# Chunked delta rule feeding a maxout FFN on one core: an earlier load and scaling of the second chunk's values, and small products moved to other places among the FFN's matmuls

## The chip, the cores and the metric

One core of one Trainium2 chip. The metric is the device time in microseconds (us) of one execution of the whole program. In the text PE is the matmul engine (TensorE), DVE the VectorE, ACT the ScalarE, POOL the GpSimd, SP the SyncE; each runs its own instructions strictly in the order in which the kernel's Python code emits them.

## The reference

A gated delta rule runs over 768 tokens for 4 x 8 heads of width 48. Its outputs are laid out as 3072 tokens of width 384 and go through a maxout FFN.

```python
k_n = k / (np.linalg.norm(k, axis=-1, keepdims=True) + 1e-06)
state = np.zeros((B, H, D, D))                  # B, H, S, D = 4, 8, 768, 48
for t in range(S):
    kt, vt, bt = k_n[:, :, t], v[:, :, t], beta[:, :, t, None]
    y[:, :, t] = np.einsum('bhd,bhde->bhe', q[:, :, t], state)
    v_old = np.einsum('bhde,bhd->bhe', state, kt)
    state = state + bt[:, :, :, None] * np.einsum('bhd,bhe->bhde', kt, vt - v_old)
x = y.transpose(0, 2, 1, 3).reshape(3072, 384)
h = np.maximum(np.maximum(x @ w1, x @ w2), x @ w3)   # w1, w2, w3: 384 x 768
out = h @ w_out                                      # w_out: 768 x 384
```

All is float32; the four FFN weights arrive as float64 and are turned into float32 on the chip.

## The kernel before, in words

**Chunks and groups.** The sequence is cut into 12 chunks `c` of 64 tokens. A chunk has two units `n = 2c + g` (g picks the batches). Two chunks make a group `m`; there are 6 groups (`GROUPS`). Within a chunk the recurrence is solved in closed form: products of keys with keys and with queries (`gram`, p_g, tiles `at` and `pt`), a triangular inverse, and a few products with the running state `st`.

**The inverse** (`solve(m)`, a generator) works on 32 x 32 blocks for a whole group: norms and beta are put together (`inverse_square`, L278 to L283, and L582), `norm` on POOL (L286 to L292) makes the key norms, one multiply over the block tile (L599, 128 x 1024) scales it, and 31 steps `j` follow of a product (L617) and a subtraction (L621) each on DVE. Each `yield` is a place where the emitting code can stop; `some(solving, n)` emits n pieces. At step `j == 1` DVE turns the norms (`norms_of`, L318). For group 0, `first_norms` has the norms of chunks 0 and 1 in `nrm_0`.

**The recurrence of chunk c** is a row of short links, each with its letter in the order tables: `e` and `f` (only in the first group) are `halves_z` (p_e, L740) and `halves_u` (p_f, L751, its negation on ACT at L755); `z` is `join_z` (p_z, L768, copies on ACT at L772); `d` is `turn_t1` (three transposes on DVE, L685 and L687); `j` is `join_u` (p_j, L781, which needs z's copies and d's transposes; ACT negates it at L783); `k` is `old_k` (p_k, L798, the state times the keys, subtracted on DVE from the scaled values `v_t` at L810); `q` is `old_q` (p_q, L798, copied by ACT at L818); `u` is `new` (p_u, L826, which needs j's result and k's); `y` is `to_y` (p_y, L868, added to q's copy on DVE at L870); `s` is `step` (p_s, L849, added into `st` on DVE at L856); `x` is `to_x` (p_x). `T` and `P` in the first table are the transposes and the score products (`gram`) of the queries of one unit, `M` a mask on DVE, `S1` one piece of `solving`.

**The values** `v_t` of a chunk come by two DMAs (`load_v`, L148) and are multiplied by the norms (`scale`, L324; on POOL for c up to 9).

**The FFN of group m** (`ffn(m)`, a generator) has products p_h (L1311), one *unit* per `yield`, followed by a copy on ACT (L1319, L1321) or a maximum on DVE (L1325), and then output products p_o (L1354; in the last three groups L1040). In group 0 a unit is 256 tokens wide. The weights are converted piece by piece meanwhile (`weights`): three ACT operations (L255 to L257) on a fetched piece, a shift on DVE (L266), an addition on POOL (L270); `fetch` (L224) issues the DMA of a piece, `join_last` emits the shift and the addition of the last piece begun. Unit number k of the first units needs piece k.

**The order.** The schedule is written out by hand. The main loops walk over the yields of `ffn(m)`, and at iteration `i` emit what the tables name: `FIRST` and `EARLY_LINKS` (with `SOLVED` for the substitution) beside `ffn(0)`, `LINKS`, `FOURTH_LINKS` and `LAST_LINKS` beside the later ones, where `X` is `turn_y` (L927, a DVE transpose that makes the next group's `xt` from outputs that went through DRAM: `y_blocks` L906 and `read_y` L916, letters x and w), `K` is `load_k` (there on the POOL queue) and `P` is `prep_values`. So moving a name to another iteration moves its place in the program order of every engine and queue that it uses.

Of the kernel before, what the change touches and what calls it, by code (L numbers as in the profile page):

```python
# [23 lines left out]
def kernel(  # L24
# [31 lines left out]
    nc = tc.nc  # L56
# [35 lines left out]
    def ps_two(name):  # L92
        return pairs.tile([128, 2, 512], FP32, name=name, tag="two", bufs=3)
# [24 lines left out]
    def rows(bb):  # L118
        return slice(C * bb, C * (bb + 1))
# [16 lines left out]
    def place(n):  # L136
        return n % NK if n < 12 else n % 4
# [4 lines left out]
    def load_q(n, queues=one_queue):  # L142
        load(q, qpad[n % NQ], n, queues)

    def load_v(c, queue=nc.sync):
        vts[c] = work.tile([128, 2, H, D], FP32, name="v_t", bufs=3)
        for bb in range(2):
            queue.dma_start(  # L148
                out=vts[c][rows(bb)].rearrange("p g h d -> p (g h) d"),
                in_=v[2 * bb : 2 * bb + 2, :, c * C : (c + 1) * C, :].rearrange(  # L150
                    "b h p d -> p (b h) d"
                ),
            )
# [78 lines left out]
    def join_last():  # L232
        if waiting:
            joined(*waiting.pop())
# [29 lines left out]
    def joined(dst, mant, mant_v, up_v):  # L264

        nc.vector.tensor_scalar(  # L266
            out=mant, in0=mant, scalar1=3, scalar2=None,
            op0=ALU.logical_shift_left,
        )
        nc.gpsimd.tensor_tensor(  # L270
            out=dst.bitcast(I32), in0=mant_v.bitcast(I32), in1=up_v, op=ALU.add
        )
# [50 lines left out]
    def scale(c, nrm):  # L323
        (nc.vector if c > 9 else nc.gpsimd).tensor_tensor(  # L324
            out=vts[c], in0=vts[c],
            in1=nrm[:, :, :, None].to_broadcast([128, 2, H, D]), op=ALU.mult,
        )
# [7 lines left out]
    nrm_0 = const.tile([128, 2, 2, H], FP32, name="nrm_0")  # L335
# [8 lines left out]
    def square(name):  # L344
        return work.tile([128, H, C], FP32, name=name, tag="square", bufs=17)
# [4 lines left out]
    def turn(n, parts=(0, 1), copy=nc.scalar.copy):  # L350

        if n not in kqts:
            if n == 6:
                kqts[n] = work.tile([128, KT, TOK], FP32, name="xt").rearrange(
                    "p k t -> p (k t)"
                )[:, 0 : NP * 4 * C].rearrange(
                    "p (j b i t) -> p j b i t", b=2, i=2, t=C
                )
            else:
                kqts[n] = work.tile([128, NP, 2, 2, C], FP32, name="kqt", bufs=6)  # L360
        kqt = kqts[n]
        p_t = ps_two("p_t")
        for i in parts:
            src = (kpad[place(n)], qpad[n % NQ])[i]
            for j in range(NP):
                nc.tensor.transpose(  # L366
                    p_t[:, i, j * 128 : (j + 1) * 128],
                    src[:, 2 * j : 2 * j + 2],
                    ident,
                )  # L370
        some = slice(parts[0], parts[-1] + 1)
        copy(  # L372
            kqt.rearrange("p j b i t -> p i (j b) t")[:, some],
            p_t.rearrange("p i (x t) -> p i x t", t=C)[:, some],
        )
# [56 lines left out]
    def gram(n, parts=(0, 1), queues=one_queue, copy=nc.scalar.copy, later=False):  # L432
        kqt, g = kqts[n], n % 2
        p_g = ps_two("p_g")

        whole = len(parts) == 2 and not g
        for j in range(NP):
            for par in range(2):
                for bb in range(2):
                    kq = kqt[dims(par), j, bb ^ g]  # L440
                    for i in (0,) if whole else parts:
                        c0 = j * 128 + i * C
                        nc.tensor.matmul(  # L443
                            p_g[
                                rows(bb ^ (g * i)), par, c0 : c0 + C * (1 + whole)
                            ],
                            kq[:, 0],
                            kq if whole else kq[:, i],
                        )
        p_v = p_g.rearrange("p two (j i t) -> p two j i t", j=NP, i=2)  # L450
        if 1 in parts:
            pt = pts[n] = square("pt")
            if later:
                return lambda: copy(by_par(pt), p_v[:, :, :, 1])
            else:
                masked(pt, p_v[:, :, :, 1])
        if 0 not in parts:
            return
        at = ats[n] = square("at")
        copy(by_par(at), p_v[:, :, :, 0])  # L460
        if queues:
            to_dram(n, queues)
# [96 lines left out]
    def solve(m):  # L559
# [34 lines left out]
        else:  # L594
            size, xv, yv = BL, x[:, None], y[:, None]
            xb, by = x, bl[:, None, :].to_broadcast([128, BL, BL])
        if m == 2:
            yield
        nc.vector.tensor_tensor(out=xb, in0=xb, in1=by, op=ALU.mult)  # L599
        yield  # L600
        for j in range(size - 1):
# [5 lines left out]
            n = BL // size  # L607
# [86 lines left out]
    def halves_t(c, parts=(0, 1)):  # L694
        if c not in fine:
            fine[c] = [square("t") for g in range(2)]
        src = [ut[c % NU][:, g].rearrange("p h x -> p (h x)") for g in range(2)]
        dst = [t.rearrange("p h x -> p (h x)") for t in fine[c]]
        if 0 in parts:
            nc.vector.transpose(out=dst[0], in_=src[0])  # L700
        for bb in range(2) if 1 in parts else ():
            nc.vector.transpose(out=dst[1][rows(1 - bb)], in_=src[1][rows(bb)])
# [684 lines left out]
    def keys(n, queues=one_queue, copy=nc.scalar.copy):  # L1387
        gram(n, (0,), queues, copy)
# [40 lines left out]
    turn(7, (0,))  # L1429
    turn(1, (1,))  # L1430
    keys(7)
    turn(2, (1,))
    gram(1, (1,), None, later=True)()
    some(conv, 1)
# [20 lines left out]
    for n in range(2):  # L1455
# [3 lines left out]
    new(0)  # L1459
    some(conv, 1)  # L1460
    fetch(nc.gpsimd)
    load_v(1, nc.gpsimd)
    placed(1, 3)
    to_y(0)
    busy(2, ident)
    join_last()
    halves_t(1)
    solving = solve(1)
    some(solving, 1)
# [7 lines left out]
    LINKS = {  # L1477
        0: "k0 q0 t0 L3", 1: "t1", 2: "g0 g1 t2", 3: "t3", 4: "z0 z1 d0 d1 V0",
        5: "g2 g3 p1", 6: "j0 j1 N0", 7: "u0 V1 N1", 8: "N2", 9: "s0 y0", 10: "x0",
        11: "k1 q1", 12: "u1 w0", 14: "y1 x1 s1", 15: "X0 w1", 16: "P0",  # L1480
        18: "X1 K0 K1 K2 K3",
    }
    FOURTH_LINKS = {
        **LINKS, 15: "w1", 16: "X0", 18: "", 19: "X1",
        21: "P0 K0 K1 K2 K3",
    }
    LAST_LINKS = {
# [11 lines left out]
    EARLY_LINKS = {  # L1499
        9: "k0 q0", 10: "t0", 11: "t1", 12: "g0", 13: "t2", 14: "g1", 15: "t3",  # L1500
        16: "g2", 17: "g3", 20: "d0 d1 z0 z1", 22: "j0", 24: "j1 u0", 26: "s0",
        28: "k1 q1", 29: "y0 u1", 30: "s1 x0", 31: "y1",
    }


    FIRST = {
        0: "S1 S1", 1: "e1 s0 S1 S1 S1", 2: "f1 k1 M2 S1 S1",
        3: "z1 d1 S1 M3 S1 S1", 4: "j1 q1", 5: "u1 T4", 6: "y1 s1 T5", 7: "x1 T6",
        8: "T7", 14: "P4", 15: "P5", 26: "P6", 27: "P7", 30: "P9 P11",
    }  # L1510


# [26 lines left out]
    def queries(names):  # L1539
# [12 lines left out]
    FETCHED = {8: 1, 12: 1, 13: 1, 14: 1, 21: 2, 22: 1, 23: 1, 24: 1, 25: 1}  # L1552
    LESS = {3: 0, 6: 1, 9: 2, 18: 3, 21: 4, 25: 5}
    SOLVED = {
        **{i + 4: n for i, n in enumerate((3, 2, 2, 2, 3, 3, 3, 3, 2, 2))},
        27: 1, 28: 1, 29: 1, 30: 6, 31: 17, 32: 6, 33: 5,
    }
    for i, _ in enumerate(ffn(0)):
        if i < 7:
            fetch(nc.sync if i else nc.gpsimd)  # L1560
        if i == 0:
            scale(1, nrm_0[:, 1])
        if i == 1:
            load_q(4)
            load_q(5)
        if i == 2:
            load_q(6)
        if i < 6 or i == 16:
            join_last()
        for _ in range(FETCHED.get(i, 0)):  # L1570
            fetch(nc.gpsimd)
        queries(FIRST.get(i, ""))
        links(1, EARLY_LINKS.get(i, ""))
        if i == 26:
            solving = solve(2)
            some(solving, 1)
        if i in CONVERTED:
            some(conv, 1 + (i == 22))
        if i == 0:
            fetch(nc.gpsimd)  # L1580
        some(solving, SOLVED.get(i, 0))
        if i in (8, 13):
            prep_values(i // 4)
        if i in (4, 8):
            for n in range(2):
                load_k(8 + 2 * (i > 4) + n, (nc.gpsimd, nc.gpsimd))
        if i == 11:
            load_q(11, (nc.gpsimd, nc.gpsimd))
        if i in (3, 9, 10, 21):
            load_v((3, 9, 10, 21).index(i) + 2)  # L1590
        if i == 18:
            blocks(2)
        if i == 30:
            prep_values(4)
        if i in (29, 30, 31):
            load_blocks(i - 17, nc.sync)
        if i in LESS:
            less_first(LESS[i], nc.gpsimd if i < 10 else nc.vector)
        if i in (30, 31):
            turn_first((2 * i - 60, 2 * i - 59))  # L1600
        if i == 31:
            turn_first((4, 5))
            for t in range(KT):
                both_layers(t)
                if t == 0:
                    links(1, "x1")
# [55 lines left out]
```

## Time and profile before

| what | before |
|---|---|
| time, median of 3 runs (lowest to highest) | 501.86 us (499.53 to 503.12) |
| the profiled execution's own time | 502.37 us |
| its span from first to last instruction | 500.7 us |
| PE busy, share of the span | 478.0 us, 95% |
| DVE, ACT, POOL busy | 348.6, 169.3, 197.9 us |
| mean granted TensorE clock | 0.981 |

The profiled execution took 1.67 us more than its span. A share of busy time is a mean over very different stretches: up to about 43 us the group 0 inverse runs and PE waits for DVE and ACT; between 43 and 70 us the first FFN units run between the links of chunk 1; from 70 us on PE is nearly always busy. A row of the timeline gives the start, the duration, the engine, the line and the tiles of one or more like instructions, and in square brackets the idle time before it with what released it.

### The profile page before, as it was taken

Reading aid. Unit: us, or ns where it says so; the run is one execution under the profiler, and the core shown is the slowest. Engines: PE = TensorE matmul, PEld = TensorE weight load, DVE = VectorE, ACT = ScalarE, POOL = GpSimd, SP = SyncE. Lnnn points to the kernel's source line nnn. Section 1 sums busy time; section 2 is a strip of 40 time slices with the busy share of each in tenths; the row PEclk is TensorE's granted clock in tenths of the full one; section 3 lists DMA queues with packets and bytes.
Section 4 is the critical chain, followed back from the end, with each engine's and each line's share of the span. In section 5 each row is a group of like instructions: output and inputs, shape, how many; then the busy total and the mean of one; then the engine's idle time right before and its main releaser. Section 6 shows DMA issues by size and latency. Waiting matters only on the chain.

```text
span 500.7 us, 18774 instructions
## 1 busy us (share of the span) xinstructions
PE 478.0 (95%) x8100; PEld 341.6 (68%) x8100; DVE 348.6 (70%) x819; ACT 169.3 (34%) x329; POOL 197.9 (40%) x334
## 2 busy tenths in 40 slices
PE   7669889999999999999999999999999999999995
PEld 6558678887765555665555564655797457998895
DVE  4888978765687361979551998565998865467843
ACT  5776755985230135111234110243211042113210
POOL 6557693864660393871574880601000020000000
PEclk9958899999999999999999999999999999999999
DMA  8948979874351654454765453833224321330001
GB/s 112 162 102 223 207 185 129 199 203 90 90 137 36 138 116 108 120 125 121 154 133 114 116 158 90 164 56 83 65 57 96 61 66 28 87 81 1 1 16 48
DMA packets 109603, 53.52 MB, mean 107 GB/s; under 512 B 92752, under 2 KB 103344, under 8 KB 109520
## 3 DMA queue, kind: packets, MB, share of 16 engines
q1 hardware_dynamic: 97824, 31.62, 31.4%
q0 software_dynamic: 9280, 20.11, 16.0%
q8 instruction: 64, 1.05, 0.9%
q10 hardware_dynamic: 2416, 0.59, 0.7%
q14 instruction: 19, 0.16, 0.1%
HBM read 39.17 MB, written 13.11 MB: 104 GB/s over the span
## 4 chain that ended last, share of the span: by engine, by line
PE 87%; DVE 8%; issue 2%; ACT 1%; DMA 1%; SPq 0%; POOL 0%; DVEq 0%; POOLq 0%; ACTq 0%
PE p_h L1311 34%; PE p_o L1040 12%; PE p_o L1354 11%; PE p_c L1249 5%; PE p_g L443 4%; PE p_u L826 3%; PE p_y L868 3%; PE p_k L798 2%; PE p_m L960 2%; PE p_q L798 2%; PE p_t L366 2%; PE p_s L849 2%; PE p_z L768 2%; PE p_j L781 2%; DVE tmp L617 2%
## 5 line engine op out<-in xcount | busy, mean ns | idle before, releaser
L1311 PE MATMUL p_h<-xt,w_sb 128*128 128x512 f32 (+1 forms) x468 | 176.8, 523 | 1.3 <-DVE tmp L617 0.9
L1311 PEld LDWEIGHTS p_h<-xt,w_sb 128*128 128x128 f32 x468 | 85.4, 191 | 64.2 <-issue 54.8
L1325 DVE TENSOR_TENSOR h<-h,p_h 128x512 f32<-128x512 f32 (+1 forms) x42 | 23.9, 569 | 44.8 <-PE p_h L1311 43.1
L621 DVE TENSOR_TENSOR y_bl<-y_bl,tmp 128x31 f32<-128x31 f32 (+20 forms) x139 | 48.6, 350 | 4.8
L617 DVE TENSOR_TENSOR tmp<-x_bl,y_bl 128x31 f32<-128x31 f32 (+20 forms) x139 | 47.0, 338 | 4.1
L1354 PE MATMUL p_o<-wo_sb,h 128*128 128x384 f32 x144 | 49.8, 491 | 0.0
L1321 ACT ACTIVATE h<-p_h 128x512 f32<-128x512 f32 (+1 forms) x30 | 16.6, 552 | 84.8 <-PE p_h L1311 80.2
L401 POOL DMA_DIRECT2D turned<-in_q_dram x72 | 39.2, 552 | 4.2 <-POOL turned L396 3.4
L1354 PEld LDWEIGHTS p_o<-wo_sb,h 128*128 128x128 f32 x144 | 26.7, 190 | 17.3
L443 PEld LDWEIGHTS p_g<-kqt 48*64 48x64 f32 x1184 | 22.7, 134 | 11.4 <-issue 7.7
L443 PE MATMUL p_g<-kqt 48*64 48x64 f32 (+1 forms) x1184 | 25.9, 234 | 2.6 <-ACT kqt L372 2.6
L270 POOL TENSOR_TENSOR w_sb<-mant,up 128x384 int32<-128x384 int32 x18 | 18.5, 1030 | 23.9 <-DVE mant L266 19.9
L396 POOL MEMSET turned<- 128x96 f32 x18 | 3.3, 189 | 56.6 <-DVE kqt L417 56.6
L653 POOL DMA_DIRECT2D ut<-y_d x4 | 2.6, 650 | 57.8 <-DMA y_d<-y_bl 57.8
L148 POOL DMA_DIRECT2D v_t<-in_v_dram x14 | 11.6, 830 | 34.5 <-PE p_u L826 34.5
L1360 ACT COPY o_sb<-p_o 128x384 f32<-128x384 f32 x12 | 5.7, 478 | 56.0 <-PE p_o L1354 50.6
L1354 PE MATMUL p_o<-w_sb,xt 128*128 128x384 f32 x60 | 21.0, 486 | 0.0
L810 DVE TENSOR_TENSOR v_t<-v_t,p_k 128x768 f32<-128x768 f32 x11 | 10.5, 950 | 15.0 <-PE p_k L798 15.0
L427 DVE TENSOR_TENSOR pt<-p_g,mask 128x512 f32<-128x512 f32 x20 | 13.6, 688 | 10.2 <-PE p_g L443 9.9
L401 POOL DMA_DIRECT2D turned<-in_k_dram x32 | 17.5, 553 | 3.3 <-DMA v_t<-in_v_dram 1.9
L460 ACT COPY at<-p_g 128x512 f32<-128x512 f32 x22 | 12.7, 583 | 17.7 <-DVE pt L427 16.2
L826 PEld LDWEIGHTS p_u<-v_t,ut 64*64 64x64 f32 x768 | 13.5, 142 | 6.7 <-issue 6.1
(254 smaller groups left out, 920.8 us busy)
## 6 DMA issues: line engine op xcount, KB each, us to landing
w_bits<-in_moe_w_dram SPq DMA_DIRECT2D x9, 384.0 KB, 5.8
w_bits<-in_moe_w_dram POOLq DMA_DIRECT2D x9, 384.0 KB, 5.4
turned<-in_q_dram POOLq DMA_DIRECT2D x72, 48.0 KB, 2.5
out_dram<-o_sb SPq DMA_DIRECT2D x34, 96.0 KB, 2.3
y_x<-y SPq DMA_DIRECT2D x30, 96.0 KB, 2.6
qall<-y_x SPq DMA_DIRECT2D x30, 96.0 KB, 2.8
v_t<-in_v_dram POOLq DMA_DIRECT2D x14, 192.0 KB, 4.6
at_d<-at SPq DMA_DIRECT2D x76, 32.0 KB, 3.0
```

The costliest lines, as they stand in the source:

```text
L270: nc.gpsimd.tensor_tensor(out=dst.bitcast(I32), in0=mant_v.bitcast(I32), in1=up_v, op=ALU.add)
L401: (queue, nc.gpsimd)[i].dma_start(out=t[p0 : p0 + 32, bb, at : at + NP * 2 * D].rearrange("p (j x) -> p j x", j=NP), in_=(k, q)[i][2 * bb ...
L443: nc.tensor.matmul(p_g[rows(bb ^ (g * i)), par, c0 : c0 + C * (1 + whole)], kq[:, 0], kq if whole else kq[:, i],)
L617: nc.vector.tensor_tensor(out=t_v, in0=row.to_broadcast(t_v.shape), in1=column.to_broadcast(t_v.shape), op=ALU.mult,)
L621: nc.vector.tensor_tensor(out=rest, in0=rest, in1=t_v, op=ALU.subtract)
L798: nc.tensor.matmul(p_b[rows(bb), par, c0 : c0 + D], kqt[g][dims(par), j, bb ^ g, i], st[dims(par), bb ^ g, g, j],)
L826: nc.tensor.matmul(p_v[rows(bb ^ g), g, i], ut[c % NU][rows(bb), g, h], rhs[rows(bb), g, h],)
L1040: nc.tensor.matmul(to[:, g], a[j][:, 128 * g : 128 * (g + 1)], b[j], start=(start and g == of[0] and j == 0), stop=(stop and g == of[-1] a ...
L1249: nc.tensor.matmul(to, w[stays], moves, start=(n == 0), stop=(n == len(terms) - 1))
L1311: nc.tensor.matmul(p_h, w_sb[i][:, t, f * 128 : (f + 1) * 128], xt[:, t, lo : lo + w], start=(t == 0), stop=(t == KT - 1),)
L1325: nc.vector.tensor_tensor(out=h, in0=h, in1=p_h, op=ALU.max)
L1354: nc.tensor.matmul(p_o, stays, moves, start=(n == 0), stop=(n == len(terms) - 1))
```

## The change

`load_v(1)` is emitted earlier and on the SP queue, behind `keys(7)`, where before it came behind `new(0)` on the POOL queue. `scale(1)` is emitted ahead of `halves_t(1)` and `solve(1)`, so on POOL it stands ahead of `norm`; before it stood in iteration 0 of the loop over `ffn(0)`. `solve(1)` gets one more place to stop, ahead of the multiply at L599, as `solve(2)` has. The tables get other places: the substitution of group 1 begins in iteration 1 instead of in `solve(1)`'s first piece and iteration 0, and is level with the old order again behind iteration 5; `k1` goes from iteration 2 to 3 (beside `z1`), `q1` from 4 to 6 (beside `y1`); `y0` of chunk 2 from 29 to 27, `P6` and `P7` from 26 and 27 to 23 and 25. In `LINKS`, `X1` and the four `K` go from iteration 18 to 17; in `FOURTH_LINKS`, `X1` goes from 19 to 18.

```diff
@@ solve(m)
-        if m == 2:
+        if m in (1, 2):
             yield
         nc.vector.tensor_tensor(out=xb, in0=xb, in1=by, op=ALU.mult)
         yield
@@ ahead of the loops
     keys(7)
+    load_v(1)
     turn(2, (1,))
     gram(1, (1,), None, later=True)()
     some(conv, 1)
...
     new(0)
     some(conv, 1)
     fetch(nc.gpsimd)
-    load_v(1, nc.gpsimd)
     placed(1, 3)
     to_y(0)
     busy(2, ident)
     join_last()
+    scale(1, nrm_0[:, 1])
     halves_t(1)
     solving = solve(1)
     some(solving, 1)
@@ LINKS, FOURTH_LINKS
-        18: "X1 K0 K1 K2 K3",
+        17: "X1 K0 K1 K2 K3",
     }
     FOURTH_LINKS = {
-        **LINKS, 15: "w1", 16: "X0", 18: "", 19: "X1",
+        **LINKS, 15: "w1", 16: "X0", 17: "", 18: "X1",
@@ EARLY_LINKS
-        28: "k1 q1", 29: "y0 u1", 30: "s1 x0", 31: "y1",
+        27: "y0", 28: "k1 q1", 29: "u1", 30: "s1 x0", 31: "y1",
@@ FIRST
-        0: "S1 S1", 1: "e1 s0 S1 S1 S1", 2: "f1 k1 M2 S1 S1",
-        3: "z1 d1 S1 M3 S1 S1", 4: "j1 q1", 5: "u1 T4", 6: "y1 s1 T5", 7: "x1 T6",
-        8: "T7", 14: "P4", 15: "P5", 26: "P6", 27: "P7", 30: "P9 P11",
+        1: "e1 S1 s0 S1 S1", 2: "f1 S1 S1 S1 M2", 3: "k1 z1 d1 S1 M3 S1 S1",
+        4: "j1", 5: "u1 T4", 6: "q1 y1 s1 T5", 7: "x1 T6",
+        8: "T7", 14: "P4", 15: "P5", 23: "P6", 25: "P7", 30: "P9 P11",
@@ SOLVED
-        **{i + 4: n for i, n in enumerate((3, 2, 2, 2, 3, 3, 3, 3, 2, 2))},
+        **{i + 4: n for i, n in enumerate((4, 3, 2, 2, 3, 3, 3, 3, 2, 2))},
@@ loop over ffn(0)
         if i < 7:
             fetch(nc.sync if i else nc.gpsimd)
-        if i == 0:
-            scale(1, nrm_0[:, 1])
```

## The prediction

> **What bounds the kernel now.** I read the page first, then the windows table by stage, then the timeline of each engine between 40 and 70 us, then PE's timeline to the end for rows with idle time.
>
> The windows table (us, then busy time and instructions of PE, PE's weight loads, DVE, ACT, POOL, then the granted clock, DMA share, GB/s):
>
> ```profile
> 50.00:55.00 5.00, 3.33 (x133) 2.72 (x132) 4.64 (x11) 2.98 (x8) 4.27 (x5) 0.97 1.11 228
> 55.00:60.00 5.00, 5.00 (x116) 3.59 (x114) 4.77 (x13) 3.79 (x8) 2.65 (x4) 0.68 1.19 209
> 60.00:65.00 5.00, 3.70 (x131) 3.01 (x128) 4.72 (x14) 4.24 (x8) 3.58 (x5) 1.00 0.77 190
> 65.00:70.00 5.00, 4.30 (x152) 3.75 (x155) 2.96 (x7) 2.96 (x6) 4.73 (x6) 1.00 0.51 114
> 75.00:80.00 5.00, 5.00 (x144) 4.31 (x143) 4.72 (x13) 1.77 (x3) 1.42 (x2) 1.00 1.35 155
> ```
>
> From 70 us to the end PE has no idle time worth naming except at 120 us (0.55 and 0.30) and at 310 us. So an order change can win only what PE loses between 43 and 70 us: 1.67 us idle in 50 to 55, 1.30 in 60 to 65, 0.70 in 65 to 70, and a clock of 0.68 in 55 to 60. DVE is busy over 4.6 of 5 us there: it has next to no slack.
>
> PE's timeline there and at 310 us:
>
> ```profile
> 48.48 0.31 PE L849 MATMUL p_s<-u,kpad 64*64 64x48 f32 x2 [0.26 <-issue]
> 51.99 1.02 PE L798 MATMUL p_k<-st,kqt 48*64 48x48 f32 x55 [0.64 <-DVE st L856]
> 54.05 0.37 PE L798 MATMUL p_k<-st,kqt 48*64 48x48 f32 x9 [1.03 <-issue]
> 54.34 2.57 PE L1311 MATMUL p_h<-xt,w_sb 128*128 128x256 f32 x6
> 60.72 0.39 PE L781 MATMUL p_j<-z,t 32*32 32x32 f32 x23 [0.68 <-issue]
> 65.70 0.68 PE L826 MATMUL p_u<-v_t,ut 64*64 64x48 f32 x30 [1.31 <-issue]
> 66.80 1.46 PE L1311 MATMUL p_h<-xt,w_sb 128*128 128x256 f32 x6
> 310.46 2.81 PE L1311 MATMUL p_h<-xt,w_sb 128*128 128x512 f32 x6 [0.87 <-DVE tmp L617]
> ```
>
> Only 0.64 us of it is a wait for another engine. Three pauses are "issue". Between them lie 126 and 127 matmuls (9 + 6 + 64 + 6 + 41, then 23 + 64 + 6 + 34), and 127 between the pause at 48.48 and the one at 54.05: a pause every 254 instructions, counting weight loads. The unit at 54.34 took 2.57 us where the one at 66.80 took 1.46.
>
> Why DVE's addition into st came late (POOL, DVE and ACT timelines):
>
> ```profile
> 42.37 1.68 POOL L148 DMA_DIRECT2D v_t<-in_v_dram  x2
> 49.39 1.47 POOL L324 TENSOR_TENSOR v_t<-v_t,nrm 128x768 f32<-128x768 f32 x1 [0.72 <-DVE y_p L621]
> 50.82 1.10 POOL L270 TENSOR_TENSOR w_sb<-mant,up 128x384 int32<-128x384 int32 x1
> 49.57 1.50 DVE L266 TENSOR_SCALAR mant<-mant 128x384 uint32<-128x384 uint32 x1
> 50.99 0.94 DVE L856 TENSOR_TENSOR st<-st,p_s 128x768 f32<-128x768 f32 x1
> 51.96 0.57 ACT L255 ACTIVATE mant<-w_bits 128x384 f32<-128x384 f32 x1 [4.04 <-POOL w_sb L270]
> ```
>
> The values were asked for at 42.37 to 44.05; L148's DMAs land in 3.7 to 6.0 us, so `scale` on POOL began at 49.39. DVE's shift, 0.35 us elsewhere, took 1.50 beside it, and L856 stood behind the shift. POOL's addition waited behind `scale`, ACT's conversion for that, and behind ACT's conversion stood the negation of p_f (53.42).
>
> **The load.** Two issues leave POOL (1.68 us) and two join SP behind the eight writes of `at` that end at 30.63; L148 on SP took 2.21 us for two. SP's next instruction, a fetch, then waited 11.4 us for its buffer, which hides the 2.2; without that cover piece 8 would come 2.2 us later. The values land by about 39 us (32.8 + 6.0). They could push the block read that POOL asks for at 36.13: ACT waited 0.6 us for it and had 0.65 us spare before its next wait. DMA share from 30 to 35 us is 0.09, so I take 0; bounds 0 and 2 us (384 KB at the 190 GB/s of the busy windows).
>
> **The scaling.** POOL's addition of piece 2, at 44.05 before, starts at 42.4, `scale` runs 43.4 to 44.9, the norm follows; its third operation waits for DVE's reciprocal (45.8) as before. L289 took 1.24 us beside the multiply L599; with the multiply put off I take 0.3, as its neighbours. POOL is free at 47.2 instead of 47.9, issues a fetch (0.8) and adds piece 3 at 48 to 49.5 instead of 50.8 to 51.9. ACT's conversion moves from 51.96 to about 49.6 and the negation from 53.42 to 51.3, right behind p_f.
>
> **k beside z.** p_s ends at 48.8; DVE now has the shift of piece 4 and the multiply done by 48.5, so st is ready at 49.8. PE reaches p_k only after the next unit, at 52.6. The 0.64 goes. With it the half clock should go: single-us windows show 0.50 from 55 to 58, after a stretch from 51.4 to 54.8 in which PE worked 1.8 of 3.4 us. That half clock cost 2.57 - 1.46 = 1.1 at 54.34 and about 0.3 in the next two groups: **1.4 us**; bounds 0 (the stretch moves on) and 1.4.
>
> **What is late next.** DVE. From 46.2 until d1's transposes are done it must run three shifts (0.35 each), two maxima (0.4), the multiply (1.15), st (0.9), steps 0 to 4 (0.4, 0.45, 0.55, 0.6, 0.65), the norm turn (0.85), a mask (0.68), one more shift, k's subtraction (0.95), d1 (1.36): 10.8 us, and about 0.8 of waits (for p_s, for ACT's conversion of piece 6): 57.8. PE without pauses would be at p_j at 56.2, with one pause of 0.5 at 56.7. So p_j waits **1.1 us**; behind it stand unit 5 and p_u. Bounds 0 (if DVE is spared its waits) and 1.6. u then needs j's negation (ACT, 1.2 us), hidden by unit 5 (1.4).
>
> **The issue pauses** (1.03 + 0.68 + 1.31 = 3.02). The number of instructions is unchanged, so pauses remain. With a DMA share of 0.2 at 120 us they were 0.55 and 0.30. 384 KB leave the window from 42 to 49 us, which moves the whole backlog up. I take 2.2 in all, **0.8 less**; bounds 0.9 (three of the quiet ones) and 5 (below). [...]
>
> **q beside y, P6, P7, y0.** No work is added. q's copy on ACT (0.80) ends under p_y (1.1) before L870 needs it; without that cover y is 0.8 later. P6, P7 and y0 lie where PE is busy 10.0 of 10 us: 0, with 0.5 either way for the two pauses at 120.
>
> **X1 and K.** At 310.46 PE waits for L927, which began at 309.11 behind three substitution steps that iteration 17 emits (3 x 0.68 us). Put ahead of them it could begin at 307.1; its data were asked for at 302.11 to 304.67, and land 2.8 us later (the median of that queue's row), by 307.5. It ends at 308.7 and the **0.87** goes; bounds 0 and 0.87. The three steps end 0 to 0.4 us later, with no one waiting. The K issues (8 on POOL, 0.69 each, by L129's row) start one iteration earlier on an engine busy under half the time: 0. In `FOURTH_LINKS` no DVE instruction stands between iterations 18 and 19: 0.
>
> **The sum**, against the profiled time: 502.37 - 0.64 - 1.4 + 1.1 - 0.8 - 0.87 = 499.8. The median of the runs lies 0.5 below the profiled one; I give **499.4**.
>
> **Rivals.** [...]
>
> [...]
>
> (3) *More comes back.* p_j does not wait, and pauses fall to the quiet 0.9: 502.37 - 0.64 - 1.4 - 0.87 - 2.1 = 497.4, 496.9 on the runs' level, less if the pauses at 120 us go too. For: DVE's waits may vanish, the DMA backlog shortens; against: DVE 4.7 of 5 us.
>
> **Chances.** Forecast 0.37, rival (1) 0.14, (2) 0.21, (3) 0.28. 1% is 5.0 us, about what a measurement of this kernel can tell from no change. Faster by more (under 496.8): 0.22 of (3) and 0.04 of the forecast, 0.26. Slower by more (over 506.9): 0.10 of (2) and 0.04 for what I do not see, 0.14. The rest, 0.60, is within 1%. The range reaches from (3) to (2): 495.8 to 505.0.
>
> **What would show it.** Right: `scale` of chunk 1 on POOL near 43.4 at 1.5 us; L856 before 50; no DVE wait ahead of p_k; a clock of 1.00 from 54 to 58; p_j waiting about 1 us for L687; the unit after the third p_o group without idle near 308. Wrong: a clock of 0.5 in another window between 56 and 70; pauses that sum to 3 us or more; PE starting its first unit later than 43.3; DVE stopping for DMA at L927.

## The result, and the profile after

The change makes the kernel slower: 504.10 us (median of 22 runs, 499.86 to 508.27) against 501.23 us (22 runs of the kernel before on the same chip, 498.23 to 504.58), a ratio of 1.0054 with a 95% interval of 1.0033 to 1.0076. The ratios here and below leave out the few executions in a slower state (three of the 22 of the change, 507.53 to 508.27 us), so they need not be the quotient of two medians. The profiled execution of the changed kernel took 504.63 us, its span 502.5; before it was 502.37 and 500.7. What follows explains these two executions, 1.8 us apart in their spans where the medians lie 2.9 us apart.

The windows table of the changed kernel (us, then busy time and instructions of PE, weight loads, DVE, ACT, POOL, then granted clock, DMA share, GB/s):

```profile
50.00:55.00 5.00, 3.57 (x119) 2.91 (x119) 4.69 (x18) 3.61 (x9) 1.80 (x2) 1.00 1.16 233
55.00:60.00 5.00, 4.48 (x126) 3.36 (x126) 4.39 (x11) 2.71 (x5) 2.91 (x3) 0.66 1.02 183
60.00:65.00 5.00, 3.77 (x116) 3.12 (x106) 4.69 (x14) 3.08 (x6) 3.28 (x5) 1.00 0.76 212
65.00:70.00 5.00, 3.80 (x156) 3.14 (x155) 4.00 (x9) 3.35 (x7) 4.64 (x6) 1.00 0.75 171
70.00:75.00 5.00, 3.75 (x50) 3.37 (x50) 2.19 (x5) 0.59 (x1) 3.24 (x5) 0.52 0.39 114
75.00:80.00 5.00, 5.00 (x26) 4.36 (x26) 3.20 (x9) 1.71 (x3) 2.20 (x3) 0.79 0.61 113
```

Between 70 and 80 us, where PE ran at full clock without a pause before, the clock is now 0.52 and 0.79, and PE is idle 1.25 us. Between 70 and 75 us DVE falls to 2.19 busy of 5 and ACT to 0.59: both wait for PE (DVE 3.4 us for p_s, ACT 5.4 us for p_t). PE's timeline names the places:

```profile
55.52 0.45 PE L798 MATMUL p_k<-st,kqt 48*64 48x48 f32 x16 [1.94 <-issue]
56.58 2.93 PE L1311 MATMUL p_h<-xt,w_sb 128*128 128x256 f32 x6
61.39 0.39 PE L781 MATMUL p_j<-z,t 32*32 32x32 f32 x24 [1.23 <-issue]
66.16 1.15 PE L798 MATMUL p_q<-st,kqt 48*64 48x48 f32 x64
67.13 1.11 PE L868 MATMUL p_y<-u,pt 64*64 64x48 f32 x64
68.41 0.56 PE L849 MATMUL p_s<-u,kpad 64*64 64x48 f32 x22 [0.16 <-ACT qs L818]
71.25 1.41 PE L849 MATMUL p_s<-u,kpad 64*64 64x48 f32 x42 [2.29 <-issue]
73.50 2.76 PE L1311 MATMUL p_h<-xt,w_sb 128*128 128x256 f32 x6
290.33 1.26 PE L826 MATMUL p_u<-v_t,ut 64*64 64x48 f32 x64 [1.12 <-POOL kmore L396]
```

No wait for DVE is left between 44 and 68 us, as intended, but the pauses called "issue" have grown from 3.28 us (the prediction's three, 3.02, and 0.26 in p_s at 48.48) to 5.46. The new one, 2.29 us, lies inside p_s, behind p_q and p_y. Behind it the unit at 73.50 takes 2.76 us at the half clock. In the kernel before p_y and p_s stood behind the unit at 66.80 and ran without a pause:

```profile
68.19 1.15 PE L868 MATMUL p_y<-u,pt 64*64 64x48 f32 x64
69.16 1.26 PE L849 MATMUL p_s<-u,kpad 64*64 64x48 f32 x64
```

Other engines of the changed kernel:

```profile
43.31 1.47 POOL L324 TENSOR_TENSOR v_t<-v_t,nrm 128x768 f32<-128x768 f32 x1
49.85 0.94 DVE L856 TENSOR_TENSOR st<-st,p_s 128x768 f32<-128x768 f32 x1
48.60 0.56 ACT L255 ACTIVATE mant<-w_bits 128x384 f32<-128x384 f32 x1 [0.21 <-POOL w_sb L270]
57.36 0.90 DVE L687 STREAM_TRANSPOSE t<-ut 32x256 f32<-32x256 f32 x2
```

The load and the scaling did what they were meant to: scaling at 43.31 instead of 49.39, st at 49.85 instead of 50.99, ACT's conversion at 48.60 instead of 51.96, and d's transposes are done at 58.26, before PE comes to p_j at 59.43.

**Where the 1.8 us of span come from.** I take four marks on PE: its first FFN unit (L1311), p_k of chunk 2 behind unit 9 of the FFN, the end of its last matmul, and the span's end. The first unit starts at 43.81 instead of 43.34: +0.47. From there to p_k of chunk 2 it takes 80.77 - 43.81 = 36.96 us instead of 76.44 - 43.34 = 33.10: **+3.86**, of which 1.68 is idle time (5.62 against 3.94, from the windows) and 2.18 longer work at a lower clock. From p_k to the last matmul 417.77 instead of 418.84: -1.07. From there to the end 3.96 instead of 5.42: -1.46. Sum 1.80. The 0.47 is no more than the scatter: with the same program up to that unit, `q_back` below started it at 44.11 and `spread` at 42.92. So the loss is in one stretch of 37 us, which I call *the stretch* below and give for each kernel, from one execution each.

### The profile page after: what moved, and what is told of

The parts are those of the page before. It is cut to its first block, busy times and chain, and to the rows that moved or that the text cites. A ratio compares the mean times of both kernels' runs of the same rounds, so it can differ in the third digit from the quotient of the medians.

```text
span 502.5 us, 18776 instructions
## 1 busy us (share of the span) xinstructions
PE 482.8 (96%) x8100; PEld 345.9 (69%) x8100; DVE 350.4 (70%) x819; ACT 169.7 (34%) x329; POOL 196.8 (39%) x332
## 4 chain that ended last, share of the span: by engine, by line
PE 86%; issue 3%; POOL 3%; DVE 3%; ACT 2%; DMA 1%; SPq 1%; ACTq 0%; POOLq 0%
PE p_h L1311 32%; PE p_o L1354 13%; PE p_o L1040 12%; PE p_c L1249 5%; PE p_g L443 4%; PE p_u L826 3%; PE p_m L960 2%; PE p_y L868 2%; PE p_k L798 2%; PE p_s L849 2%; PE p_q L798 2%; PE p_j L781 2%; POOL turned L401 2%; PE p_z L768 2%; PE p_t L366 1%
## 5 line engine op out<-in xcount | busy, mean ns | idle before, releaser
L1311 PE MATMUL p_h<-xt,w_sb 128*128 128x512 f32 (+1 forms) x468 | 178.8, 527 | 0.3 <-ACT xt L894 0.3
L1311 PEld LDWEIGHTS p_h<-xt,w_sb 128*128 128x128 f32 x468 | 86.2, 193 | 63.1 <-issue 53.7
L617 DVE TENSOR_TENSOR tmp<-x_bl,y_bl 128x31 f32<-128x31 f32 (+20 forms) x139 | 50.7, 365 | 4.1
L621 DVE TENSOR_TENSOR y_bl<-y_bl,tmp 128x31 f32<-128x31 f32 (+20 forms) x139 | 46.5, 334 | 4.8
L443 PEld LDWEIGHTS p_g<-kqt 48*64 48x64 f32 x1184 | 24.2, 143 | 11.0 <-issue 6.9
L443 PE MATMUL p_g<-kqt 48*64 48x64 f32 (+1 forms) x1184 | 27.6, 243 | 2.0 <-ACT kqt L372 2.0
L148 POOL DMA_DIRECT2D v_t<-in_v_dram x12 | 9.9, 830 | 33.7 <-PE p_u L826 33.7
L856 DVE TENSOR_TENSOR st<-st,p_s 48x768 f32<-48x768 f32 (+1 forms) x18 | 17.1, 948 | 3.8 <-PE p_s L849 3.4
L810 DVE TENSOR_TENSOR v_t<-v_t,p_k 128x768 f32<-128x768 f32 x11 | 10.5, 951 | 11.7 <-PE p_k L798 11.7
```

Source lines behind the costliest of these rows:

```text
L443: nc.tensor.matmul(p_g[rows(bb ^ (g * i)), par, c0 : c0 + C * (1 + whole)], kq[:, 0], kq if whole else kq[:, i],)
L617: nc.vector.tensor_tensor(out=t_v, in0=row.to_broadcast(t_v.shape), in1=column.to_broadcast(t_v.shape), op=ALU.mult,)
L621: nc.vector.tensor_tensor(out=rest, in0=rest, in1=t_v, op=ALU.subtract)
L856: nc.vector.tensor_tensor(out=s_v[r], in0=s_v[r], in1=p_s[r, :, 0 : H * D], op=ALU.add)
L1311: nc.tensor.matmul(p_h, w_sb[i][:, t, f * 128 : (f + 1) * 128], xt[:, t, lo : lo + w], start=(t == 0), stop=(t == KT - 1),)
```

## The experiments

Ratios are to runs of the kernel before on the same chip, with 95% intervals.

**Which part loses.** Four kernels. In `front_alone` the late tables are as before:

```diff
-        17: "X1 K0 K1 K2 K3",
+        18: "X1 K0 K1 K2 K3",
-        **LINKS, 15: "w1", 16: "X0", 17: "", 18: "X1",
+        **LINKS, 15: "w1", 16: "X0", 18: "", 19: "X1",
-        27: "y0", 28: "k1 q1", 29: "u1", 30: "s1 x0", 31: "y1",
+        28: "k1 q1", 29: "y0 u1", 30: "s1 x0", 31: "y1",
-        8: "T7", 14: "P4", 15: "P5", 23: "P6", 25: "P7", 30: "P9 P11",
+        8: "T7", 14: "P4", 15: "P5", 26: "P6", 27: "P7", 30: "P9 P11",
```

> The change without its late tables: LINKS, FOURTH_LINKS, y0 of chunk 2, P6 and P7 stand as before; load, scaling, substitution, k and q of chunk 1 as changed. Theory A (instruction blocks: PE stops every 254 instructions until a block is there, some 5 to 6 us after the last boundary, and q, y, s in a row meet two boundaries within 3 us): the whole loss is here, about 504 (ratio to before 1.006), with 'issue' pauses of some 5 us between 50 and 75 us, one of over 1.5 us inside p_s, and the granted clock at half in a window behind it; the wait of p_h near 310 us is there again. Theory C (the late tables lose the time, through the turn of y put ahead of the last substitution steps): about 501, ratio 1.000.

Measured: 505.36 us, ratio 1.0077 (1.0043 to 1.0112); the stretch 37.61 us, pauses 1.22, 2.75 and 1.67 (in p_s). All of the loss is in the front. `late_alone` is the reverse: the kernel before with those four lines as changed.

> The kernel before with the late tables alone (X1 and K one iteration earlier, y0 of chunk 2, P6, P7). Theory A: within 1 us of before, 500.5 to 502; the 0.87 us near 310 goes, and a wait of p_u of about 1 us near 287 takes its place. Theory C: 503 to 504, and PE's idle time after 100 us grows by 2 us or more.

Measured: 500.83 us, 0.9978 (0.9946 to 1.001): no loss, at best a small gain. The wait near 310 us is gone, and p_u waits 1.12 us at 288. `q_back` is the change with one name put back:

```diff
-        4: "j1", 5: "u1 T4", 6: "q1 y1 s1 T5", 7: "x1 T6",
+        4: "j1 q1", 5: "u1 T4", 6: "y1 s1 T5", 7: "x1 T6",
```

> The change with q1 back at iteration 4 beside j1; everything else as changed. Theory A: the boundary then lies under p_u as before and not in q, y, s; the pause of 2.3 us in p_s falls under 0.5 us, no half clock after 70 us, 499.5 to 501.5 (ratio about 0.999). Theory B (the pauses grow because the values and the weights are asked for earlier and crowd the DMA queues, whatever the order of the matmuls): still about 504 with 5 us of pauses.

Measured: 502.46 us, 1.0008 (0.9979 to 1.0037); the stretch 33.98 us. No pause in p_s and no half clock after 70 us; behind a pause of 2.85 us in p_j the clock was at half from 60.6 to 67.4 us. The loss is gone, though the time misses the 499.5 to 501.5 expected: the two other pauses still sum to 4.06 us. `values_alone` is the kernel before with the load on SP and the scaling ahead of the norm, tables and substitution as before:

```diff
     keys(7)
+    load_v(1)
...
-    load_v(1, nc.gpsimd)
...
     join_last()
+    scale(1, nrm_0[:, 1])
     halves_t(1)
...
-        if i == 0:
-            scale(1, nrm_0[:, 1])
```

> The kernel before with only the load of the values on SP and their scaling ahead of the norm; substitution, k, q and all tables as before. Theory A: the wait of p_k for DVE goes, pauses stay at 3 us, 499.5 to 501 (ratio 0.997 to 1.000). Theory B: 503 to 504, with pauses of 5 us.

Measured: 502.01 us, 1.0004 (0.9975 to 1.0034); the stretch 33.52. In its timeline of PE:

```profile
53.49 0.37 PE L798 MATMUL p_k<-st,kqt 48*64 48x48 f32 x9 [1.61 <-issue]
61.15 0.39 PE L781 MATMUL p_j<-z,t 32*32 32x32 f32 x23 [2.25 <-issue]
```

p_k no longer waits for DVE, but the two pauses end at 53.49 and 61.15, where they ended at 54.05 and 60.72 before. In `front_alone` they end at 54.65 and 61.69, in `q_back` at 55.08 and 61.23. PE comes to the same place earlier and goes on at nearly the same time. The pauses came to 3.86 us, where 3 or 5 were expected. Theory B falls: the early load does not lengthen the whole.

**What the pause is.** `shift32` puts matmuls that are used for nothing into two idle places of PE near 12 and 19 us:

```diff
     some(solving, 1)
+    busy(8, ident)
     keys(4)
...
+    busy(8, ident)
     turn(1, (1,))
     keys(7)
```

> The change with 16 matmuls on the identity (32 in the records) put into PE's idle places near 12 and 19 us; they compute nothing that is used. Theory A (PE stops every 254 instructions): the pauses come 32 recorded matmuls earlier in the order: after about 16 of p_k, 8 of p_j, and near the end of p_y (54) instead of 48, 40 and 22 of p_s. A wait for data or for a buffer would stay at its place (48, 40, 22). Time within 2 us of the change.

PE's timeline of it:

```profile
55.10 0.45 PE L798 MATMUL p_k<-st,kqt 48*64 48x48 f32 x16
57.11 0.92 PE L798 MATMUL p_k<-st,kqt 48*64 48x48 f32 x48 [1.56 <-issue]
60.13 0.50 PE L781 MATMUL p_j<-z,t 32*32 32x32 f32 x8
62.20 0.69 PE L781 MATMUL p_j<-z,t 32*32 32x32 f32 x56 [1.56 <-issue]
69.82 1.00 PE L868 MATMUL p_y<-u,pt 64*64 64x48 f32 x54
73.20 0.37 PE L868 MATMUL p_y<-u,pt 64*64 64x48 f32 x9 [2.38 <-issue]
```

The pauses moved by exactly 32 recorded matmuls, to 16 of p_k, 8 of p_j and 54 of p_y. So they hang on the count of instructions and on no data or buffer. (Two more pauses, 0.90 and 1.26 us, came before the first unit, which started at 46.25.) The page of the changed kernel has the other side of it, the larger of two queues that carry instructions:

```profile
q8 instruction: 63, 1.03, 0.9%
```

63 packets for 16,200 matmuls and weight loads are 257 instructions each: PE takes its program in blocks. That it stops at a boundary until the next block is there shows in the times of these packets: between 43 and 130 us the 16 traces of this case have 65 such pauses on PE, and every one ends 1.2 to 1.8 us after the end of a packet on q8; the nine in the traces of the kernel before and of the change end 1.34 to 1.70 us after it. For the pause in p_s of the changed kernel the packet moved from 67.95 to 69.81, and PE went on at 71.25. The time of `shift32` was 504.76 us, 1.0052 (1.0017 to 1.0087), as the change; the stretch 35.83.

**Is it the data transfers that hold the blocks up?** `early_in_after` moves transfers of the change out of the crowded time:

```diff
     keys(7)
     load_v(1)
+    load_v(2)
+    load_q(4)
     turn(2, (1,))
+    load_q(5)
...
     turn(3, (1,))
+    load_q(6)
...
-        if i == 1:
-            load_q(4)
-            load_q(5)
-        if i == 2:
-            load_q(6)
...
-        if i in (3, 9, 10, 21):
-            load_v((3, 9, 10, 21).index(i) + 2)
+        if i in (9, 10, 21):
+            load_v((9, 10, 21).index(i) + 3)
```

> The change, with the values of chunk 2 and the queries of units 4, 5 and 6 asked for right behind load_v(1), when the DMA queues are nearly idle (30 to 40 us), instead of at iterations 1 to 3 (45 to 58 us); order of all else as changed. Theory A1 (the blocks of instructions come late because data transfers crowd the queues from 45 to 65 us): the pauses in p_k, p_j and p_s fall from 5.5 us to under 2.5 in sum, the second pause ends before 60 us, and the time falls by 3 us or more against the change, to 499 to 501 (ratio to before 0.995 to 1.000). Theory D (a block comes 5 to 7 us after the last boundary whatever else the queues carry): pauses and time as in the change, ratio 1.005.

The windows and two rows of PE's timeline:

```profile
55.00:60.00 5.00, 4.33 (x195) 3.48 (x186) 4.76 (x13) 4.56 (x9) 3.41 (x4) 1.00 0.34 109
60.00:65.00 5.00, 4.99 (x109) 3.94 (x103) 4.72 (x13) 4.82 (x9) 2.30 (x4) 1.00 0.32 92
65.00:70.00 5.00, 2.29 (x128) 2.08 (x128) 4.76 (x12) 1.68 (x4) 4.66 (x7) 1.00 0.90 189
```

```profile
55.98 0.45 PE L798 MATMUL p_k<-st,kqt 48*64 48x48 f32 x16 [0.37 <-issue]
71.03 1.41 PE L849 MATMUL p_s<-u,kpad 64*64 64x48 f32 x42 [3.36 <-issue]
```

With the DMA share down to 0.34 and 0.32 the pause in p_k fell to 0.37, the one in p_j vanished and one of 0.40 came in p_q, but the one in p_s grew to 3.36 (share 0.90 there). The pause in p_q, 22 matmuls into it, stands on the boundary that the changed kernel crossed without a stop. Time 504.04, 1.0045 (1.0014 to 1.0075): no gain that can be told; theory A1 holds for two pauses and fails for the time. `early_in_before` makes the same four moves on top of `values_alone`.

> The kernel before with the values of chunk 1 on SP and scaled early, and with the same early requests of the values of chunk 2 and of three units of queries; all tables as before. Theory A1: pauses between 50 and 70 us fall from 3.9 us (with the values alone) to under 1.5, no half clock after 50 us, 497 to 499.5 (ratio 0.990 to 0.996). Theory D: as with the values alone, ratio 1.000.

Measured: 500.59 us, 0.9987 (0.9961 to 1.0013). The stretch fell to 32.23 us, but PE came to its first unit at 45.20; on the way it paused 1.06 us in a p_u at 39 us, where the moved transfers now run, and pauses of 1.69 in p_s and 1.59 in p_k remain, where under 1.5 in sum were expected. `more_dma` adds transfers to the kernel before:

```diff
+        if i in (1, 2, 3):
+            extra = dram.tile([128, H * D], FP32, name="extra", bufs=3)
+            for bb in range(2):
+                nc.sync.dma_start(
+                    out=extra[rows(bb)].rearrange("p (h d) -> p h d", d=D),
+                    in_=v[bb, :, 0:C, :].rearrange("h p d -> p h d"),
+                )
```

> The kernel before with six more transfers of 96 KB, in runs of 192 bytes, from an input to unused DRAM, asked for on SP in iterations 1 to 3; order of the engines' work as before. Theory A1: the pauses between 50 and 70 us grow from 3.0 us to 5 us or more, the time to 503.5 to 506 (ratio 1.004 to 1.010). Theory D: pauses 3 us, ratio 1.000 to 1.002.

Measured: 501.01 us, 1.0002 (0.9977 to 1.0026), the stretch 33.16. Its pauses in the stretch sum to 4.54 us, but no half clock followed them in its profile (the units at 73.92 and 75.65 took 1.46 us each, as at full clock), and the time is unchanged. The added transfers raised the DMA share from 65 to 70 us from 0.51 to 1.11, and PE paused 1.58 us in p_s in the old order too. So crowding lengthens single pauses, but brought no loss in the order before. How much of the pause in p_s it makes in the new order no run separates: none has quiet queues there.

**The one move.** `q_alone` is the kernel before with q1 moved:

```diff
-        4: "j1 q1", 5: "u1 T4", 6: "y1 s1 T5", 7: "x1 T6",
+        4: "j1", 5: "u1 T4", 6: "q1 y1 s1 T5", 7: "x1 T6",
```

> The kernel before with one name moved: q1 from iteration 4 to 6, ahead of y1 and s1. Theory E (a block of 254 instructions is there no sooner than some 4 us after the last boundary, and 5 to 6.5 us where data transfers crowd; so a stretch whose 128 matmuls take less makes PE stop): boundaries in p_j, in p_q and in p_s; from the one in p_q to the one in p_s PE has 128 small matmuls, 2.1 us of work, and stops 2 to 3.5 us in p_s, with a half clock after it: 503.5 to 505 (ratio 1.004 to 1.008), the loss of the whole change from this one move. Rival F (it takes the changed substitution and k as well, which leave DVE late for y): ratio 1.000 to 1.002.

PE's timeline:

```profile
68.59 1.15 PE L798 MATMUL p_q<-st,kqt 48*64 48x48 f32 x64
69.56 1.11 PE L868 MATMUL p_y<-u,pt 64*64 64x48 f32 x64
70.82 0.56 PE L849 MATMUL p_s<-u,kpad 64*64 64x48 f32 x23 [0.15 <-ACT qs L818]
74.23 1.40 PE L849 MATMUL p_s<-u,kpad 64*64 64x48 f32 x41 [2.85 <-issue]
76.47 2.77 PE L1311 MATMUL p_h<-xt,w_sb 128*128 128x256 f32 x6
```

The same pause in the same place, then the same half clock. Time 507.85 us (6 runs), 1.0123 (1.008 to 1.0166), more than the whole change; the stretch 37.20. Its profiled execution also reached the first unit only at 46.36, before anything that differs. `q_in_values` makes the same move on top of `values_alone`, to tell the two apart.

> The kernel with the values of chunk 1 early (ratio 1.000 to before) and q1 moved from iteration 4 to 6, nothing else. Theory E: the stretch from the first FFN unit to p_k of chunk 2 grows from 33.5 to 37 us through a pause of 2 to 3.5 us in p_s and a half clock behind it; ratio 1.006 to 1.009. If the loss of the one move is really 1.2% (as measured when it was made alone, in an execution whose first 12 us also ran at half clock), ratio 1.010 or more, and something besides this stretch must be longer.

Measured: 506.68 us, 1.0079 (1.0044 to 1.0114), against 1.0004 without the move; a pause of 3.36 us in p_s, the stretch 36.96. In its timeline of PE:

```profile
74.94 0.84 PE L849 MATMUL p_s<-u,kpad 64*64 64x48 f32 x41 [3.36 <-issue]
```

So the move costs about 3.8 us by the ratios, 3.4 by the stretch. Both kernels of this pair had the half clock for 3.4 us of the stretch, so here the loss is the pauses alone: 7.23 us in sum against 3.86. Why `q_alone` lost some 2 us more is open.

**Spreading the small matmuls.** `spread` is the change with

```diff
-        4: "j1", 5: "u1 T4", 6: "q1 y1 s1 T5", 7: "x1 T6",
+        4: "j1", 5: "q1 u1 T4", 6: "y1 T5", 7: "s1 x1 T6",
```

> The change with q1 at iteration 5 ahead of u1, y1 at 6 and s1 at 7 with x1: never more than 128 small matmuls between two FFN units. Theory E: boundaries in p_k, p_j, p_u and then in or behind p_s, 5.6 us of work after the one in p_u: no pause there, pauses in p_k and p_j as in the change (3 us), up to 1.5 in p_u; 500 to 502 (ratio 0.998 to 1.002). Rival F: as the change, 1.005.

Measured: 502.79 us, 1.0022 (0.9989 to 1.0056), the stretch 33.71; pauses of 1.40 in p_k and 2.30 in p_j, none behind. Rival F falls: k and the substitution are as in the change, and the loss in the stretch is gone; the interval of the time alone would still allow the change's 1.0054. `spread_early` also asks early for two units of queries (load_q(4) behind load_v(1), load_q(5) behind turn(2), none in iteration 1).

> As 'spread', and the queries of units 4 and 5 asked for right behind load_v(1) (192 KB each) instead of in iteration 1. Theory E: 384 KB fewer between 45 and 52 us bring the block for p_k nearer, its pause falls under 1 us; 499 to 501 (ratio 0.995 to 1.000), if the start of the first FFN unit stays within 0.5 us of the change's.

Measured: 502.41 us, 0.9977 (0.9943 to 1.001), the stretch 33.35; the pause in p_k fell to 0.67 and the one in p_j to 1.20, but the first unit started 1.3 us later than in the change, and the time gains nothing that can be told. `values_late` joins `values_alone` and `late_alone`, and `best` adds those early queries.

> The kernel before with the values of chunk 1 early and the late tables, but substitution, k and q of chunk 1 as before. Theory E: gains of the two parts add, 499.5 to 501 (ratio 0.996 to 0.999); p_k without a wait for DVE, pauses 3 to 4 us, none over 0.5 us in p_s. Rival (the late tables cost by the later block tile near 287 us): ratio 1.001 to 1.003.

> Values of chunk 1 early, the late tables as changed, substitution, k and q as before, and the queries of units 4 and 5 asked for right behind load_v(1). Theory E: pauses between 50 and 70 us under 2.5 us in sum, no wait near 310 us; 499 to 500.5, ratio 0.994 to 0.998. If the early queries only move the crowding to an earlier block (a pause of some 1 us in p_u near 39 us was seen with more of them early), ratio 0.998 to 1.001.

Measured: 501.37 us, 1.0008 (0.997 to 1.0046), and 502.29 us, 1.0014 (0.9982 to 1.0046), both above the times expected. `best` has the shortest stretch of all, 31.20 us, but reached its first unit at 46.17. No version tried is faster than the kernel before by more than its interval.

**All stretches together.** With q, y and s in a row: 36.96, 37.61, 35.04 (`early_in_after`), 35.83, 37.20, 36.96. Without: 33.10, 33.85, 33.98, 33.52, 32.23, 33.16, 33.71, 33.35, 33.33, 31.20. The two sets don't overlap, whatever else differs.

## Why the prediction was wrong, point by point

**The step that failed** is "q beside y ... No work is added", costed at nothing. The cover that it named held: y's addition waited only 0.16 us for ACT's copy of q. What it left out is where the boundaries between blocks fall. It had counted the 254 instructions, and treated the pauses as a sum that stays or shrinks ("I take 2.2 in all, 0.8 less"). They came to 5.46. A boundary falls some 23 matmuls into p_q, at about 66.5 us, and the next 22 into p_s; between them lie some 127 small matmuls, done at 68.97. PE went on at 71.25, 4.7 us after the boundary. Over all kernels the time from one boundary to the end of the next pause was 3.8 to 4.0 us where the queues were quiet (124.20 to 128.02 in `early_in_after`, and the two rows below of the kernel before, with a DMA share of 0.03 from 118 to 126 us) and up to 7.7 (53.49 to 61.15 in `values_alone`).

```profile
120.56 0.27 PE L798 MATMUL p_k<-st,xt 48*64 48x48 f32 x3 [0.55 <-issue]
124.56 0.96 PE L868 MATMUL p_y<-u,pt 64*64 64x48 f32 x50 [0.30 <-issue]
```

So even with quiet queues I estimate a pause of 1.3 us in p_s: 3.8 less the 2.5 us of work behind the boundary. In the old order that piece of program had an FFN unit and T4 in it and took 3.9 us (65.70 to about 69.6), so in that execution there was nothing to wait for; `late_alone` and `more_dma`, in the same order, paused there 0.48 and 1.58 us.

The chances gave 0.14 to rival (1) and 0.21 to rival (2), the slow end of the range. No run shows what the bound of 5 us on the pauses and the upper end of 505.0 were estimated from; the change had 5.46 us of pauses, 2.18 us of longer work at a lower clock and 504.10 us. Where it lost them is the pause inside p_s and the half clock behind it.

**The half clock** was to go (1.4). It stayed from 55 to 60 (0.66 after, 0.68 before), now behind the 1.94 us pause in p_k, and came again from 70 to 77 us behind the pause in p_s; windows of 1 us at its start and end (the granted clock is third from the right):

```profile
70.00:71.00 1.00, 0.00 (x0) 0.00 (x0) 0.00 (x0) 0.00 (x0) 0.92 (x1) 0.62 0.76 191
77.00:78.00 1.00, 1.00 (x9) 0.97 (x8) 0.90 (x4) 0.59 (x1) 0.42 (x1) 0.97 0.35 60
```

By windows of 1 us the time at half clock here is 6.8 us. It accounts for the 2.18 us of longer work: the unit at 73.50 alone took 2.76 us where the one at 66.80 took 1.46 before. How much half clock follows such a pause differs between the traces: by windows of 5 us 6.8 us in `q_alone` as in the change, 3.4 in `q_in_values`; `early_in_after` reads 0.51 from 70 to 75 us. In `front_alone` the unit behind it, at 74.87, took 2.33 us, in `shift32`, at 76.20, 1.79 (1.46 at full clock). What starts it and what sets its length no run shows: `more_dma` had 4.54 us of pauses without it.

**The wait of p_k for st** (0.64) went, as worked out. It gained nothing: in `values_alone` the pauses took it. **p_j's wait for DVE** (1.1) did not come, because the unit ahead ran at half clock and d was done first, at 58.26 (57.8 was given). In `spread`, where that unit ran at full clock, PE came to p_j at 56.85 and waited 0.25, until 57.31; DVE ended d at 57.63, close to the time given. What was too large is the wait: p_j went on before all of d was done. **The load and the scaling**: scaling, st and the negation of p_f came within 0.1 us of the times given, ACT's conversion 1 us earlier. **X1**: the 0.87 went; but the transpose now holds up the substitution's last steps, the block tile of the next group comes later, DVE waits for it 7.0 instead of 5.3 us, and p_u waits 1.12 us at 290 (the row names POOL; DVE's subtraction for it, L810, ended at 290.23, just before p_u began). The prediction had said that no one waits. That chain is read from the two traces and was not tried by itself; the late tables together cost nothing. **The pauses at 120 us** (0.85) went, which was left at 0.5 either way.

**A reading that was off.** DVE was not busy over 4.6 of 5 us from 65 to 70 us (2.96). That moves no term of the sum.

## What to carry to other kernels

Where a profile shows an engine idle for "issue" at a regular count of instructions, count the instructions between two such places and the time that they take: a run of many short instructions can cost more than its busy time if it spans two boundaries, here by a pause of 1.67 to 3.36 us. Put long instructions between short ones so that each block lasts as long as the next one takes to come, here 3.8 to 7.7 us, and look up where the boundaries fall before moving a group past a long instruction. A wait that is removed ahead of such a boundary may gain nothing, as in `values_alone`, and a stop of 2.29 us was followed here by 6.8 us at half clock, with 2.18 us of longer work in that stretch.

## What the runs showed of the hardware

PE's program came in blocks of 254 to 257 instructions (254 between two pauses, 257 to a packet of q8 in the changed kernel); a pause ended 3.8 to 7.7 us after the boundary before, with little other traffic still 3.8 to 4.0, and 1.2 to 1.8 us after the block's own packet. From 72 us on the changed kernel shows no such pause; at the boundaries inside small matmuls it had 5.46 us of them, and other runs up to 3.36 at once. The stays at half clock that began between the first FFN unit and p_k of chunk 2 lasted, by windows of 1 or 5 us, 3.4 us in the kernel before, `spread`, `q_in_values` and `best`, 3.4 and 6.8 in the change, twice 3.4 in `values_late`, 6.8 in `q_alone` and `spread_early`; `more_dma` had none. I had also not expected that a whole execution can reach its first FFN unit 3 us later: at 46.36 in `q_alone`, whose program up to there is that of the kernel before (43.34), and at 46.43 in `q_in_values` against 43.62 in `values_alone`. The traces show where it arises: the first groups of p_g, which took 0.69 to 0.70 us before, took 1.13 to 1.14 in `q_alone`, `q_in_values` and `best`, and p_g behind them began at 15.77 to 16.07 us instead of 13.29. That looks like the half clock, and the expectation of `q_in_values` calls it so, but the windows from 0 to 15 us read a granted clock of 1.00; the cause stays open.
